# Two more operand sets, scans in place and a product tile of half the size in a chunked recurrence, with the inverse's contractions tied to steps

## The chip, the core and the metric

The kernel runs on one core of a Trainium2 chip. The metric is the device time of one execution in microseconds. The core's engines work side by side, each through its own instructions in order: TensorE (PE, with its weight loads shown as PEld), VectorE (DVE), ScalarE (ACT), GpSimd (POOL) and SyncE (SP), whose queue issues most of the DMAs. An instruction that waits holds up everything behind it on its engine or queue.

## The reference

A recurrence over 768 tokens for 4 batches of 8 heads with head dimension 40, and behind it a mixture of experts over all 3072 tokens.

```python
state = np.zeros((B, H, D, D), dtype=np.float32)
for t in range(S):
    y[:, :, t] = np.einsum('bhd,bhde->bhe', rt, state)
    Sa = np.einsum('bhde,bhe->bhd', state, at)
    state_decay = state * wt[:, :, None, :] - np.einsum('bhd,bhe->bhde', Sa, bt)
    state = state_decay + np.einsum('bhd,bhe->bhde', vt, kt)
...
x = np.ascontiguousarray(attn_out.transpose(0, 2, 1, 3)).reshape(B * S, H * D)
...
P = np.exp(logits)                      # logits = x @ w_gate, less the maximum
for _ in range(8):
    P /= P.sum(1, keepdims=True) + 1e-09
    P /= P.sum(0, keepdims=True) + 1e-09
    P *= N / E
for e in range(E):
    h = np.maximum(x @ w1[e], 0.0)
    ye = h @ w2[e]
    out += P[:, e:e + 1] * ye
```

## The kernel before

The recurrence is cut into 12 chunks of 64 tokens (c = 0 to 11). Within a chunk the dependence of one token on the next is solved by a triangular inverse, so that a chunk becomes a few small matrix products; only the state passes from chunk to chunk. Four pieces of work make up this stage.

**prep(c, b)** (L116 to L179) makes the operands of one chunk of one batch, 48 times in all; below, n = 4c + b is a prep's number. It loads the packed input into a tile inp (L119; from n = 8 on from a pool of two buffers), scans the running product of the decays forwards into q (L123, DVE), takes a reciprocal (L128) and scans backwards into gf (L133, DVE). gf goes out to memory as gd (L137, SP) and is read back later. POOL (for n of 8 and more) multiplies kb (L147) and the two halves of ab (L153, L154). TensorE forms the products ll (L159) and the transposes kt (L167), and ScalarE and VectorE copy the results into one of NSX = 20 operand sets: sx (L155, L156, L169, L174) and bb (L175, L176), with a small cc (L152). ScalarE also copies the strictly triangular part to lt (L173), which goes out to memory as ld (L178, on ScalarE's queue). Set n is used again by prep n + 20, so its tiles can be overwritten when step 3 of the recurrence of n has read bb.

**The inverse** of a pair of chunks (a segment s; eight preps belong to it) runs on VectorE. load_lu brings the eight ld back as lu, one small matrix in each partition (L367). inv_diag (L181) builds the inverses of the 8-wide diagonal blocks in seven short steps. inv_off (L198) joins two blocks of n with two products; contract (L189) makes each in two instructions, a multiply with the whole three-fold product into the tile pr (L193) and a sum over one index (L196). There are two joins of 8-blocks, of 512 products each, and one join of 16-blocks, done in four contractions of 2048, 1024, 1024 and 2048 products, so eight contractions in all. finish (L353) copies the inverse once transposed into pr (L356) and stores both as ud and nd (L358, L359).

**tload and tmat** read the pieces of the inverse for one chunk (L222 to L231, SP) and compute its remaining block with TensorE (gp L241, op L246) into tt.

**recur(c, b)** (L250) is the recurrence itself, a generator with five steps: loads of v, r, gr and vt (L253 to L259, SP), av and f (L269, DVE); xc (L276, PE) and its copies; pu (L287) and pm (L289, DVE), which need tt; c (L294, PE), ws (L296, DVE), y (L300, POOL) and z (L311, POOL until chunk 8, then DVE); and the transposed state vz (L316 to L319) for the next chunk. ScalarE also copies z into the next f (L264). Two buffers of y are stored as xd (L304).

**What sets the order.** Every piece gets an event time (L371 to L407), in which one step of the recurrence is one unit: step k of (c, b) stands at 5c + k + 1.1b. The instructions are traced in the order of these times, and a list scheduler with a timeline model then orders each engine: where an engine would be free it takes the ready instruction that was traced first, so that ready work with a late event time can be drawn forward into a gap. A segment that begins with chunk c0 has its preps from 5 c0 - 18 on, 0.75 apart, its load_lu right behind the last, and then the parts of the inverse 0.05 apart, so practically all at once. tload of a chunk stands at 5c - 0.5.

The recurrence ends at about 520 us; then the mixture of experts (from L476 on) fills TensorE. Its pools take over the memory of the recurrence's. pmat, ones and ident, which its normalization uses, have memory of their own throughout.

Of the kernel before, what the change touches and what calls it, by code (L numbers as in the profile page):

```python
# [11 lines left out]
F32 = mybir.dt.float32  # L12
# [17 lines left out]
def attention(ctx, tc, d, xd, ps, pq, pt, gs, lg):  # L30
    nc = tc.nc
    pin = ctx.enter_context(tc.tile_pool(name="a_in", bufs=1))
    inv = ctx.enter_context(tc.tile_pool(name="a_inv", bufs=1))
    sets = [ctx.enter_context(tc.tile_pool(name=f"a_set{i}", bufs=1)) for i in range(NSX)]
    const = ctx.enter_context(tc.tile_pool(name="a_const", bufs=1))
# [2 lines left out]
    dr = ctx.enter_context(tc.tile_pool(name="a_dr", bufs=2, space=bass.MemoryType.DRAM))  # L38
    dr1 = ctx.enter_context(tc.tile_pool(name="a_dr1", bufs=1, space=bass.MemoryType.DRAM))

    cst = const.tile([128, 64 + 64 + 104 + 128 + 40 + 260], F32, name="cst")
    nc.sync.dma_start(out=cst, in_=d["cst"])
    mask_u = cst[0:64, 0:64]
    mask_f = cst[0:R2, 64:128]
    mask_p = cst[:, 128:232]
    ident = cst[:, 232:360]
    one65 = cst[0:RP, 400:660]

    NTB = 2
    sx_b, bb_b, cc_b = ([None] * NSX for _ in range(3))  # L50
    raws = {}
    for n in range(NCH * NB - NSX, NCH * NB):
        i, pool = n % NSX, sets[n - NCH * NB + NSX]
# [20 lines left out]
    c1_b = [const.tile([R2, NP, 104], F32, name=f"c1{i}") for i in range(2)]  # L74
    unf = inv.tile([128, 1056], F32, name="un")
    luf = inv.tile([128, 1056], F32, name="lu")
    prf = inv.tile([128, 2048], F32, name="pr")
    gtf = inv.tile([128, 256], F32, name="gt")
    un, lu, tn = (t[:, 0:1024].rearrange("u (a b) -> u a b", b=32) for t in (unf, luf, prf))
    und, lud = (t.rearrange("u (b x) -> u b x", x=264)[:, :, 0:256].rearrange("u b (c j) -> u b c j", j=32)  # L80
# [19 lines left out]
    def first_use(i):  # L100
        if i in fresh:
            fresh.discard(i)
            nc.gpsimd.memset(bb_b[i], 0.0)
            nc.scalar.copy(out=sx_b[i][64:128].rearrange("r p h x -> r (p h) x")[:, :, 64:104],
                           in_=cst[64:128, 360:400].unsqueeze(1).broadcast_to([64, 8, 40]))

    state = {"sx": 0, "ab": 0, "g1": 0, "vz": 0, "c1": 0, "tt": 0, "f": 0, "rb": 0, "x1": 0}

# [7 lines left out]
    def prep(c, b, ld):  # L116
        cb = c * NB + b
        inp = raws[IN_MAP[cb]][0:RP, 0:1029] if IN_MAP.get(cb) else pin.tile([RP, 1029], F32, name="inp", bufs=2)
# [5 lines left out]
            out=qf.rearrange("r p t -> r (p t)"), data0=inp[:, 0:260], data1=one65,  # L124
# [4 lines left out]
        sx = rot("sx", sx_b)  # L129
        i = next(j for j in range(NSX) if sx_b[j] is sx)  # L130
        bb, cc = bb_b[i], cc_b[i]
        gf = pin.tile([RP, NP, 65], F32, name="gf", bufs=2)
        nc.vector.tensor_tensor_scan(  # L133
            out=gf.rearrange("r p t -> r (p t)")[:, 259::-1], data0=inp[:, 260:0:-1],
            data1=g1.rearrange("r p t -> r (p t)")[:, 259::-1], initial=0.0, op0=ALU.mult, op1=ALU.add)
        gd[c, b] = dr1.tile([RP, 260], F32, name=f"gd{cb}")
        nc.sync.dma_start(out=gd[c, b], in_=gf.rearrange("r p t -> r (p t)"))  # L137
        g = gf[0:R2, :, 64:0:-1]
        if cb < NKB:
            raw = raws[KB_SETS[cb % len(KB_SETS)]]  # L140
            kb = raw[0:R2, 0:512].rearrange("r (p k t) -> r p k t", p=NP, k=2)
            lt = raw[0:64, 512:1024].rearrange("r (p k t) -> r p k t", p=NP, k=2)
        else:
            kb = kb1
            lt = pin.tile([64, NP, 2, 64], F32, name="lt")
        eng = nc.vector if cb < NFAST else nc.gpsimd
        (nc.gpsimd if cb in KB_POOL else eng).tensor_tensor(  # L147
            out=kb[0:R2], in0=kb_in,
# [17 lines left out]
        for p in range(NP):  # L166
# [3 lines left out]
            out=sx[0:64, :, :, 0:64], in0=ll[0:64],  # L170
# [18 lines left out]
    def contract(us, dst, a, m):  # L189
        nu = us.stop - us.start  # L190
        n_c, n_r, n_k = a.shape[1], m.shape[2], a.shape[2]
        prv = prf[us, 0:n_c * n_r * n_k].rearrange("u (c k r) -> u c k r", r=n_r, k=n_k)
        nc.vector.tensor_tensor(  # L193
            out=prv, in0=a.unsqueeze(3).broadcast_to([nu, n_c, n_k, n_r]),
            in1=m.unsqueeze(1).broadcast_to([nu, n_c, n_k, n_r]), op=ALU.mult)
        nc.vector.tensor_reduce(out=dst, in_=prv.rearrange("u c k r -> u c r k"), op=ALU.add, axis=AX.X)  # L196

    def inv_off(us, o, n, h):  # L198
        gt = gtf[us, 0:n * n].rearrange("u (c r) -> u c r", r=n)
        un_, lu_ = un[us], lu[us]  # L200
        if h == n:
            contract(us, gt, un_[:, o:o + n, o:o + n], lu_[:, o:o + n, o + n:o + 2 * n])
            contract(us, un_[:, o:o + n, o + n:o + 2 * n], gt, un_[:, o + n:o + 2 * n, o + n:o + 2 * n])
            return
        contract(us, gt[:, 0:h], un_[:, o:o + h, o:o + n], lu_[:, o:o + n, o + n:o + 2 * n])
        contract(us, gt[:, h:n], un_[:, o + h:o + n, o + h:o + n], lu_[:, o + h:o + n, o + n:o + 2 * n])
        contract(us, un_[:, o:o + n, o + n:o + n + h], gt[:, :, 0:h], un_[:, o + n:o + n + h, o + n:o + n + h])
        contract(us, un_[:, o:o + n, o + n + h:o + 2 * n], gt, un_[:, o + n:o + 2 * n, o + n + h:o + 2 * n])

    INV = [(inv_diag, (i,)) for i in range(1, 8)] + [(inv_off, a) for a in ((0, 8, 8), (16, 8, 8), (0, 16, 8))]  # L210

    def tload(c):
        tt = rot("tt", tt_b)
# [36 lines left out]
    def recur(c, b):  # L250
# [9 lines left out]
                          in_=d["vt"][c, b].rearrange("s (g x) -> s g x", x=40))  # L260
# [6 lines left out]
        for p in range(NP):  # L267
            nc.tensor.matmul(av[:, p], lhsT=vz[:, p], rhs=rb[:, p], start=True, stop=True)
        nc.vector.tensor_tensor(  # L269
            out=f[0:R2, :, :, 0:64], in0=av,  # L270
# [28 lines left out]
        y = ys[c, b // 2]  # L299
        nc.gpsimd.tensor_tensor(out=y[:, :, b % 2], in0=ws[:, :, 0:64], in1=gr[0:R2, :, 64:0:-1], op=ALU.mult)  # L300
# [9 lines left out]
        z = wk.tile([R2, NP, 40], F32, name="z", bufs=4)  # L310
# [36 lines left out]

    def warm():
        fl = pt.tile([128, 512], F32, name="fl", tag="pt")
        for _ in range(4):  # L350
            nc.tensor.matmul(fl, lhsT=unf[:, 384:512], rhs=cst[:, 0:512], start=True, stop=True)

    def finish(s, us):  # L353
        if not s:
# [16 lines left out]
    ev = [(T_CLEAR, clear, ())]  # L371
# [11 lines left out]
    for c in range(NCH):  # L383
# [3 lines left out]
        t = 5 * c + 2 - T_LEAD  # L387
# [3 lines left out]
    for s, cs in enumerate(GROUPS):  # L391
        us = slice(0, 64 * len(cs))
        t0 = 5 * cs[0] - 10
        n = len(cs) * NB
        for i in range(n):
            cb = (cs[0] + i // NB, i % NB)
            j = cb[0] * NB + cb[1] - NSX
            t = 5 * (j // 4) + 3 + SKEW * (j % 4) + 0.01
            t = max(t, t0 + P0 + PD * i) if s else -20 + 0.01 * i
            ev.append((t, do_prep, (s,) + cb + (i == 0,)))  # L400
        t += 0.02
        ev.append((t, load_lu, (s, len(cs))))
        for i, (fn, a) in enumerate(INV):
            ev.append((t + INV_DT * i, fn, (us,) + a))
        ev.append((t + INV_DT * 10 + 0.01, finish, (s, us)))
    for _, fn, args in sorted(ev, key=lambda x: x[0]):
        fn(*args)  # L407
    while gq:
# [5 lines left out]
GRP = {c: (i, j) for i, g in enumerate(GROUPS) for j, c in enumerate(g)}  # L414
P0 = -8
PD = 0.75
INV_DT = 0.05
SKEW = 1.1
NSX = 20
GL = 1  # L420
NY = 2
NGR = 2
NFB = 3
NRB = 2
KB_POOL = (1,2,3,4,5,6,7)
IN_SETS = (19, 18, 17, 16)
KB_SETS = (15, 14, 13, 12)
IN_SEQ = (19,18,17,16,0,0,19,18)
IN_MAP = dict(enumerate(IN_SEQ))
N_SP = 8  # L430
NKB = 8
# [23 lines left out]
def body(ctx, tc, d, out):  # L455
    nc = tc.nc
# [2 lines left out]
    xv = xd.rearrange("(k r) (s u c) -> s u r k c", k=2, u=3, c=256)  # L459

    one = ctx.enter_context(tc.tile_pool(name="one", bufs=1))
    pmat = one.tile([128, 24, E], F32, name="pmat")
    lg = one.tile([128, 24, E], F32, name="lg")
    ones = one.tile([128, 128], F32, name="ones")
    ident = one.tile([128, 128], F32, name="ident")
    gs = one.tile([R2, NP, E], F32, name="gs")

    with ExitStack() as actx:
        ps, pq, pt = (actx.enter_context(tc.tile_pool(name=f"a_ps{i}", bufs=n, space=bass.MemoryType.PSUM))
                      for i, n in enumerate((PC, PQ, PT)))  # L470
        nc.sync.dma_start(out=gs, in_=d["gate"])
        attention(actx, tc, d, xd, ps, pq, pt, gs, lg)
        nc.gpsimd.memset(ones, 1.0)
        nc.sync.dma_start(out=ident, in_=d["cst"][:, 232:360])

    stg = ctx.enter_context(tc.tile_pool(name="stg", bufs=2))  # L476
    x0 = ctx.enter_context(tc.tile_pool(name="x0", bufs=1))
    hp = ctx.enter_context(tc.tile_pool(name="hp", bufs=2))
# [279 lines left out]
def _layout(inputs):  # L758
# [18 lines left out]
    x = split(g["r"])  # L777
# [14 lines left out]
    wg = g["moe_w_gate"].reshape(NP, 2, D, E).transpose(1, 2, 0, 3)  # L792
    gate = np.zeros((R2, NP, E), np.float32)
    gate[0:40], gate[64:104] = wg[0], wg[1]
    cst = np.zeros((128, 660), np.float32)
    i = np.arange(64)
    up = (i[:, None] < i[None, :]).astype(np.float32)
    cst[0:64, 0:64] = up
    cst[0:64, 64:128] = up
    cst[64:128, 64:128] = 1.0  # L800
    cst[0:64, 128:192] = up
    cst[64:128, 128:192] = up
    cst[:, 192:232] = 1.0
    cst[:, 232:360] = np.eye(128)
    cst[64:104, 360:400] = np.eye(40)
    cst[:, 400::65] = 1.0
# [20 lines left out]
```

## Time and profile before

| | us |
|---|---|
| median of 3 runs | 1840.97 |
| lowest and highest | 1838.9 and 1845.11 |
| the profiled execution's own time | 1844.61 |
| its span in the profile | 1842.7 |
| VectorE idle, 193 to 238 us | 0.15 |
| VectorE idle, 238 to 268 us | 14.47 |

A line of a group reads: source line, engine, operation, tile written and tiles read, shapes, count, then busy time and mean ns, then the idle time before it and what ended that. A line of a timeline begins with start and duration in us. A line of the waits gives who waited for whom, the total in us, how often, and the longest. A row of a stretch gives from and to, the length, and per engine the busy time and in brackets the count of instructions, then the granted TensorE clock, the share of DMA and GB/s. A line of the chain gives start, length and what it was.

### The profile page before, as it was taken

To read this page: it belongs to the slowest core of one execution; us is meant where nothing else is said; L and a number is where in the kernel's file an instruction comes from. 1 tells how busy PE (TensorE), PEld (TensorE's weight loads), DVE (VectorE), ACT (ScalarE), POOL (GpSimd) and SP (SyncE) were. 2 spreads that over 40 slices of the span, in tenths; PEclk is the share of its full clock that TensorE was granted. 3 is DMA by queue.
4 is the path that set the end of the run, shared out by engine and by line. 5 is a ranking of instruction groups with operands and counts; after the bars stand their busy time and mean duration, and the time that the engine had idled before them with its cause. 6 is when DMAs were issued, how large, how long until landed. Compare 5 with 4: busy or idle time off the path is not lost.

```text
span 1842.7 us, 31504 instructions
## 1 busy us (share of the span) xinstructions
PE 1732.1 (94%) x11851; PEld 1697.6 (92%) x11851; DVE 1387.3 (75%) x2319; ACT 856.0 (46%) x1848; POOL 857.4 (47%) x844
## 2 busy tenths in 40 slices
PE   5488888899989999999999999999999999999999
PEld 4378888888889999999999999999999999999999
DVE  8876968877688768677776868977686877777676
ACT  6346667665643534344343433445343443425342
POOL 6545545532662617355371826007191744628170
PEclk8579899999899999999999999999999999999999
DMA  8467887875820102011110202201020111102001
GB/s 215 128 151 165 188 182 184 183 175 130 207 74 31 57 4 71 22 53 39 37 58 17 76 19 69 65 12 57 19 75 20 56 38 38 57 19 75 6 33 43
DMA packets 194957, 145.10 MB, mean 79 GB/s; under 512 B 143861, under 2 KB 171637, under 8 KB 194805
## 3 DMA queue, kind: packets, MB, share of 16 engines
q1 hardware_dynamic: 189013, 137.09, 28.7%
q10 hardware_dynamic: 5792, 6.00, 1.2%
q8 instruction: 94, 1.54, 0.3%
q14 instruction: 58, 0.48, 0.1%
HBM read 117.00 MB, written 26.04 MB: 78 GB/s over the span
## 4 chain that ended last, share of the span: by engine, by line
PE 73%; DVE 13%; DMA 7%; issue 3%; ACT 2%; POOL 1%; SPq 1%; ACTq 0%; DVEq 0%; POOLq 0%
PE op L636 36%; PE p L571 33%; DVE pr L193 2%; DVE un L196 2%; DMA inp<-in_inp_dram 2%; DVE gt L196 1%; DVE q L123 1%; DMA ld<-lt 1%; DMA lu<-ld 1%; DVE gf L133 1%; DMA td<-nd 1%; PE pu L287 1%; PE ll L159 1%; DMA rb<-in_r_dram 1%; DVE pm L289 1%
## 5 line engine op out<-in xcount | busy, mean ns | idle before, releaser
L571 PE MATMUL p<-xch,wh 128*128 128x384 f32 (+1 forms) x1792 | 604.8, 339 | 8.9 <-DVE sm L589 5.2
L592 ACT ACTIVATE hh<-sm 128x384 fp32r<-128x384 f32 x512 | 269.5, 527 | 725.3 <-DVE sm L589 725.3
L636 PE MATMUL op<-wh,hh 128*128 128x320 f32 x1536 | 476.8, 311 | 1.0 <-ACT hh L592 0.9
L636 PE MATMUL op<-wl,hh 128*128 128x320 f32 x1536 | 474.7, 310 | 0.0
L636 PE MATMUL op<-wh,hl 128*128 128x320 f32 x1536 | 467.3, 310 | 0.8 <-DVE hl L595 0.8
L517 POOL TENSOR_TENSOR wl<-ws,wh 128x640 fp32r<-128x640 f32 x60 | 103.0, 1716 | 608.3 <-ACT wh L515 608.2
L595 DVE SCALAR_TENSOR_TENSOR hl<-sm,hh 128x384 fp32r<-128x384 f32 x512 | 371.1, 758 | 2.4 <-ACT hh L592 2.0
L571 PEld LDWEIGHTS p<-xch,wh 128*128 128x128 f32 (+1 forms) x1792 | 337.2, 188 | 12.6 <-DVE sm L589 6.3
L571 PE MATMUL p<-xcl,wh 128*128 128x384 f32 x896 | 302.5, 338 | 0.0
L571 PE MATMUL p<-xch,wl 128*128 128x384 f32 x896 | 301.7, 337 | 0.0
L636 PEld LDWEIGHTS op<-wh,hh 128*128 128x128 f32 x1536 | 290.2, 189 | 1.6 <-ACT hh L592 1.5
L636 PEld LDWEIGHTS op<-wl,hh 128*128 128x128 f32 x1536 | 291.0, 189 | 0.0
L636 PEld LDWEIGHTS op<-wh,hl 128*128 128x128 f32 x1536 | 287.2, 188 | 1.1 <-DVE hl L595 1.0
L589 DVE TENSOR_TENSOR sm<-p,u 128x384 f32<-128x384 f32 x384 | 233.1, 617 | 8.8
L589 DVE TENSOR_TENSOR sm<-p,p 128x384 f32<-128x384 f32 x128 | 71.3, 557 | 129.8 <-PE p L571 76.3
L571 PEld LDWEIGHTS p<-xcl,wh 128*128 128x128 f32 x896 | 168.7, 188 | 0.0
L571 PEld LDWEIGHTS p<-xch,wl 128*128 128x128 f32 x896 | 168.6, 188 | 0.0
L589 DVE TENSOR_TENSOR p<-p,p 128x384 f32<-128x384 f32 x128 | 71.2, 556 | 102.6 <-PE p L571 102.2
L589 DVE TENSOR_TENSOR u<-p,p 128x384 f32<-128x384 f32 x128 | 70.9, 554 | 59.4 <-PE p L571 58.2
L525 POOL TENSOR_TENSOR wl<-ss,wh 128x512 fp32r<-128x512 f32 x60 | 89.7, 1496 | 28.3 <-ACT wh L522 24.2
L300 POOL TENSOR_TENSOR y<-ws,gr 104x256 f32<-104x256 f32 x48 | 47.1, 980 | 113.1 <-DVE ws L296 99.9
L700 DVE SCALAR_TENSOR_TENSOR acc<-op,pmat,acc 128x320 f32<-128x320 f32 x168 | 91.3, 544 | 4.5 <-PE op L636 4.4
(160 smaller groups left out, 2717.4 us busy)
## 6 DMA issues: line engine op xcount, KB each, us to landing
ws<-in_wts_dram SPq DMA_DIRECT2D x60, 832.0 KB
inp<-in_inp_dram SPq DMA_DIRECT2D x42, 450.2 KB
rb<-in_r_dram SPq DMA_DIRECT2D x48, 224.0 KB
gd<-gf SPq DMA_DIRECT2D x48, 113.8 KB
gr<-gd SPq DMA_DIRECT2D x48, 113.8 KB
vz<-in_v_dram SPq DMA_DIRECT2D x48, 112.0 KB
ld<-lt ACTq DMA_DIRECT2D x40, 128.0 KB
f<-in_vt_dram SPq DMA_DIRECT2D x48, 80.0 KB
```

What stands on the lines that cost most here:

```text
L123: nc.vector.tensor_tensor_scan(out=qf.rearrange("r p t -> r (p t)"), data0=inp[:, 0:260], data1=one65, initial=0.0, op0=ALU.mult, op1=ALU.add)
L193: nc.vector.tensor_tensor(out=prv, in0=a.unsqueeze(3).broadcast_to([nu, n_c, n_k, n_r]), in1=m.unsqueeze(1).broadcast_to([nu, n_c, n_k, n_ ...
L196: nc.vector.tensor_reduce(out=dst, in_=prv.rearrange("u c k r -> u c r k"), op=ALU.add, axis=AX.X)
L300: nc.gpsimd.tensor_tensor(out=y[:, :, b % 2], in0=ws[:, :, 0:64], in1=gr[0:R2, :, 64:0:-1], op=ALU.mult)
L517: g.tensor_tensor(out=wl[:, 0:640], in0=raw[:, 256:896], in1=wh[:, 0:640], op=ALU.subtract)
L525: g.tensor_tensor(out=lv[:, 3:7], in0=so[:, :, 0], in1=hv[:, 3:7, 0], op=ALU.subtract)
L571: nc.tensor.matmul(o, lhsT=w_, rhs=x_, start=(j == 0), stop=(j == 3))
L589: eng.tensor_tensor(out=out, in0=x, in1=y, op=ALU.add)
L592: nc.scalar.activation(out=hh[:, f, h], in_=sm[f][:, h], func=AF.Relu)
L595: v.scalar_tensor_tensor(out=hl[:, f, h], in0=sm[f][:, h], scalar=0.0, in1=hh[:, f, h], op0=ALU.max, op1=ALU.subtract)
L636: nc.tensor.matmul(ops[i], lhsT=a[:, h, cs], rhs=w_[:, cw], start=(f == 0 and h == 0 and j == 0), stop=(last and h == 1 and j == 2))
L700: nc.vector.scalar_tensor_tensor(out=acc[:, m], in0=ops[i], scalar=pmat[:, n, e:e + 1], in1=acc[:, m], op0=ALU.mult, op1=ALU.add)
```

## The change

- NSX goes from 20 to 22. The sets that lend their memory to the first preps (IN_SETS, KB_SETS, IN_SEQ) move along.
- Room for them: the backward scan writes in place into inp, so gf is a part of inp, and gd is stored from there. From n = 8 on lt lies in inp too, over the k and b that kb has been made of. The product tile pr goes from 2048 to 1024 columns. Two masks become one, and the identity of the first use of a set is cut from the large one. pmat, ones and ident get memory only after the recurrence; the load of ident and the fill of ones move behind it.
- The joins of the inverse are ten contractions, each with at most 1024 products: four for the joins of 8, and six for the join of 16 (1024, 768, 1024, 1024, 768, 1024).
- Their event times are spread. From the second segment on they lie 0.44 units apart for the first four and 0.94 for the last six; the last stands 7.2 units behind load_lu and finish 7.9 behind it.
- From the second segment on, ahead of each contraction, `after` copies one element of a z into a corner of pr. It is the z of the latest step that stands at least one unit earlier in the event list, if there is one. Since the contraction writes pr, it can't be put ahead of that copy, nor the copy ahead of that z.

```diff
-    prf = inv.tile([128, 2048], F32, name="pr")
+    prf = inv.tile([128, 1024], F32, name="pr")
...
-        gf = pin.tile([RP, NP, 65], F32, name="gf", bufs=2)
+        gf = inp[:, 1:261].rearrange("r (p t) -> r p t", p=NP)
         nc.vector.tensor_tensor_scan(
-            out=gf.rearrange("r p t -> r (p t)")[:, 259::-1], data0=inp[:, 260:0:-1],
+            out=inp[:, 260:0:-1], data0=inp[:, 260:0:-1],
...
-        nc.sync.dma_start(out=gd[c, b], in_=gf.rearrange("r p t -> r (p t)"))
+        nc.sync.dma_start(out=gd[c, b], in_=inp[:, 1:261])
...
-            lt = pin.tile([64, NP, 2, 64], F32, name="lt")
+            lt = inp[0:64, 261:773].rearrange("r (p k t) -> r p k t", p=NP, k=2)
...
+        m, e = o + n, o + 2 * n
+        if part:
+            contract(us, un_[:, o:m, m + x:m + y], gt[:, :, 0:y], un_[:, m:m + y, m + x:m + y])
+        else:
+            contract(us, gt[:, x:y], un_[:, o + x:o + y, o + x:m], lu_[:, o + x:m, m:e])
+
+    INV = [(0.06 * i, inv_diag, (i,)) for i in range(1, 8)]
+    INV += [(0.5 + 0.35 * i, inv_off, (o, 8, 0, 8, i % 2)) for i, o in enumerate((0, 0, 16, 16))]
+    INV += [(2.0 + 0.75 * i, inv_off, (0, 16, x, y, i // 3))
+            for i, (x, y) in enumerate(((0, 4), (4, 8), (8, 16), (0, 8), (8, 12), (12, 16)))]
...
+        zs[c, b] = z
...
+    def after(t):
+        at = {5 * c + 3 + SKEW * b: z for (c, b), z in zs.items() if 5 * c + 3 + SKEW * b <= t - GATE}
+        if at:
+            nc.vector.tensor_copy(out=prf[0:1, 0:1], in_=at[max(at)][0:1, 0, 0:1])
...
-            nc.tensor.matmul(fl, lhsT=unf[:, 384:512], rhs=cst[:, 0:512], start=True, stop=True)
+            nc.tensor.matmul(fl[:, 0:296], lhsT=unf[:, 384:512], rhs=cst[:, 0:296], start=True, stop=True)
...
-        for i, (fn, a) in enumerate(INV):
-            ev.append((t + INV_DT * i, fn, (us,) + a))
-        ev.append((t + INV_DT * 10 + 0.01, finish, (s, us)))
+        for dt, fn, a in INV:
+            ti = t + dt * (INV_DT if s else 0.1)
+            if s and fn is inv_off:
+                ev.append((ti - 0.001, after, (ti,)))
+            ev.append((ti, fn, (us,) + a))
+        ev.append((t + 6.3 * (INV_DT if s else 0.1), finish, (s, us)))
...
-INV_DT = 0.05
+INV_DT = 1.25
+GATE = 1.0
 SKEW = 1.1
-NSX = 20
+NSX = 22
...
+    mid = ctx.enter_context(tc.tile_pool(name="mid", bufs=1))
+    pmat = mid.tile([128, 24, E], F32, name="pmat")
+    ones = mid.tile([128, 128], F32, name="ones")
+    ident = mid.tile([128, 128], F32, name="ident")
+    nc.gpsimd.memset(ones, 1.0)
+    nc.sync.dma_start(out=ident, in_=d["cst"][:, 168:296])
```

More of the change, by code (lines that the diff above doesn't have):

```diff
@@ L39, in attention @@
     dr1 = ctx.enter_context(tc.tile_pool(name="a_dr1", bufs=1, space=bass.MemoryType.DRAM))
-    cst = const.tile([128, 64 + 64 + 104 + 128 + 40 + 260], F32, name="cst")
+    cst = const.tile([128, 64 + 104 + 128 + 260], F32, name="cst")
     nc.sync.dma_start(out=cst, in_=d["cst"])
     mask_u = cst[0:64, 0:64]
[L44 to L47, printed above, removed]
+    mask_f = cst[0:R2, 0:64]
+    mask_p = cst[:, 64:168]
+    ident = cst[:, 168:296]
+    one65 = cst[0:RP, 296:556]
     NTB = 2
@@ L104, in first_use @@
             nc.scalar.copy(out=sx_b[i][64:128].rearrange("r p h x -> r (p h) x")[:, :, 64:104],
-                           in_=cst[64:128, 360:400].unsqueeze(1).broadcast_to([64, 8, 40]))
+                           in_=ident[64:128, 64:104].unsqueeze(1).broadcast_to([64, 8, 40]))
     state = {"sx": 0, "ab": 0, "g1": 0, "vz": 0, "c1": 0, "tt": 0, "f": 0, "rb": 0, "x1": 0}
@@ L196, in contract, with inv_off @@
         nc.vector.tensor_reduce(out=dst, in_=prv.rearrange("u c k r -> u c r k"), op=ALU.add, axis=AX.X)
-    def inv_off(us, o, n, h):
+    def inv_off(us, o, n, x, y, part):
         gt = gtf[us, 0:n * n].rearrange("u (c r) -> u c r", r=n)
         un_, lu_ = un[us], lu[us]
[L201 to L210, printed above, removed]
+        m, e = o + n, o + 2 * n
[7 more added lines that the diff above has]
+            for i, (x, y) in enumerate(((0, 4), (4, 8), (8, 16), (0, 8), (8, 12), (12, 16)))]
     def tload(c):
@@ L338, in gate_step @@
                 gq.popleft()
+    zs = {}
+    def after(t):
+        at = {5 * c + 3 + SKEW * b: z for (c, b), z in zs.items() if 5 * c + 3 + SKEW * b <= t - GATE}
+        if at:
+            nc.vector.tensor_copy(out=prf[0:1, 0:1], in_=at[max(at)][0:1, 0, 0:1])
     gq, gcount = deque(), [0]
@@ L349, in warm @@
         fl = pt.tile([128, 512], F32, name="fl", tag="pt")
-        for _ in range(4):
-            nc.tensor.matmul(fl, lhsT=unf[:, 384:512], rhs=cst[:, 0:512], start=True, stop=True)
+        for _ in range(7):
+            nc.tensor.matmul(fl[:, 0:296], lhsT=unf[:, 384:512], rhs=cst[:, 0:296], start=True, stop=True)
     def finish(s, us):
@@ L425 @@
 KB_POOL = (1,2,3,4,5,6,7)
-IN_SETS = (19, 18, 17, 16)
-KB_SETS = (15, 14, 13, 12)
-IN_SEQ = (19,18,17,16,0,0,19,18)
+IN_SETS = (21, 20, 19, 18)
+KB_SETS = (17, 16, 15, 14)
+IN_SEQ = (21, 20, 19, 18, 0, 0, 21, 20)
 IN_MAP = dict(enumerate(IN_SEQ))
@@ L461, in body @@
     one = ctx.enter_context(tc.tile_pool(name="one", bufs=1))
-    pmat = one.tile([128, 24, E], F32, name="pmat")
     lg = one.tile([128, 24, E], F32, name="lg")
-    ones = one.tile([128, 128], F32, name="ones")
-    ident = one.tile([128, 128], F32, name="ident")
     gs = one.tile([R2, NP, E], F32, name="gs")
@@ L472, in body @@
         attention(actx, tc, d, xd, ps, pq, pt, gs, lg)
-        nc.gpsimd.memset(ones, 1.0)
-        nc.sync.dma_start(out=ident, in_=d["cst"][:, 232:360])
+    mid = ctx.enter_context(tc.tile_pool(name="mid", bufs=1))
[4 more added lines that the diff above has]
+    nc.sync.dma_start(out=ident, in_=d["cst"][:, 168:296])
     stg = ctx.enter_context(tc.tile_pool(name="stg", bufs=2))
@@ L794, in _layout @@
     gate[0:40], gate[64:104] = wg[0], wg[1]
-    cst = np.zeros((128, 660), np.float32)
+    cst = np.zeros((128, 556), np.float32)
     i = np.arange(64)
@@ L798, in _layout @@
     cst[0:64, 0:64] = up
+    cst[64:128, 0:64] = 1.0
     cst[0:64, 64:128] = up
[L800 to L806, printed above, removed]
+    cst[64:128, 64:128] = up
+    cst[:, 128:168] = 1.0
+    cst[:, 168:296] = np.eye(128)
+    cst[:, 296::65] = 1.0
     arrays = dict(inp=inp, r=rb.reshape(NCH, NB, RP, NP, 128), v=packed(g["v"]),
```

## Prediction

> **What bounds the kernel now.** I read the page's head first, then the table by stretch, then the groups of VectorE by shape, then the timelines of single engines around one prep.
>
> ```profile
> span 1842.7 us, 31504 instructions
> ```
>
> The execution took 1844.61 us, so 1.9 us lie around this span; the median of the three runs, 1840.97, is 3.6 us below it. The mixture of experts behind about 520 us is full of TensorE work and the change does not touch its code. So the question is the recurrence, from about 110 to 500 us. Its rows give per stretch: length, then busy time and count of PE, PEld, DVE, ACT and POOL, then granted clock, DMA share and GB/s.
>
> ```profile
> 110.00:157.00 47.00, 43.10 (x380) 40.55 (x381) 41.73 (x53) 29.38 (x74) 27.23 (x26) 0.85 0.70 159
> 193.00:238.00 45.00, 41.27 (x382) 39.16 (x383) 44.85 (x60) 31.76 (x81) 24.21 (x29) 0.93 0.81 185
> 238.00:268.00 30.00, 24.60 (x236) 22.87 (x235) 15.53 (x34) 20.19 (x51) 12.75 (x20) 0.93 0.83 176
> 268.00:313.00 45.00, 40.94 (x380) 38.67 (x380) 44.97 (x60) 30.96 (x79) 23.85 (x30) 0.93 0.80 189
> 313.00:343.00 30.00, 24.65 (x236) 23.12 (x236) 15.92 (x35) 20.56 (x52) 12.57 (x20) 0.93 0.86 183
> 343.00:387.00 44.00, 38.87 (x374) 36.62 (x373) 43.97 (x58) 30.04 (x76) 23.41 (x29) 0.97 0.79 185
> 387.00:412.00 25.00, 23.71 (x237) 22.05 (x237) 11.96 (x30) 18.10 (x47) 6.80 (x11) 1.00 0.74 159
> 410.00:443.00 33.00, 32.16 (x310) 29.86 (x309) 32.83 (x35) 18.63 (x48) 7.78 (x9) 0.95 0.50 113
> ```
>
> The pattern repeats every 75 us, once for each pair of chunks: 45 us in which VectorE has no idle time at all (44.85 of 45), because the whole inverse lies there, and 30 us in which it is half idle (15.53 of 30). The stretch 387 to 412 shows what TensorE does with less in its way: 237 matmul records in 25 us, 9.48 a us. The bursts reach 382 / 45 = 8.49, the quiet stretches 236 / 30 = 7.87. So neither half runs at TensorE's pace; the burst is bound by VectorE. In the quiet half the wait that stands out is VectorE's for the prep's input, between 120 and 500 us (total, times, longest):
>
> ```profile
> DVE q L123 <- DMA inp<-in_inp_dram: 20.7, 6, 5.2
> ```
>
> **Part 1, the smaller product tile.** These are the eight instructions of the block of 16 (mean ns stands behind the bar and the busy time), and the small copy that is nearest to the tie:
>
> ```profile
> L196 DVE TENSOR_REDUCE un<-pr 128x128 f32<-128x2048 f32 x5 | 19.2, 3846 | 0.0
> L196 DVE TENSOR_REDUCE gt<-pr 128x128 f32<-128x2048 f32 x5 | 18.2, 3631 | 0.0
> L193 DVE TENSOR_TENSOR pr<-un,lu 128x2048 f32<-128x2048 f32 x5 | 12.2, 2450 | 0.0
> L193 DVE TENSOR_TENSOR pr<-gt,un 128x2048 f32<-128x2048 f32 x5 | 11.4, 2277 | 0.0
> L196 DVE TENSOR_REDUCE un<-pr 128x128 f32<-128x1024 f32 x5 | 9.9, 1985 | 0.0
> L196 DVE TENSOR_REDUCE gt<-pr 128x128 f32<-128x1024 f32 x5 | 9.5, 1893 | 0.0
> L193 DVE TENSOR_TENSOR pr<-un,lu 128x1024 f32<-128x1024 f32 x5 | 6.5, 1302 | 0.0
> L193 DVE TENSOR_TENSOR pr<-gt,un 128x1024 f32<-128x1024 f32 x5 | 6.0, 1209 | 0.0
> L330 DVE COPY lg<-lp 128x8 f32<-128x8 f32 x21 | 3.2, 151 | 0.5 <-PE lp L326 0.5
> ```
>
> The eight sum to 18.59 us. The new code has six contractions, four of 1024 products and two of 768. A pair of 1024 is 1.30 + 1.89 = 3.19 us. From 2048 to 1024 a multiply falls by 1.12 ns an element and a reduce by 1.70, so a pair of 768 is 3.19 - 256 x 2.82 ns = 2.47. Together 4 x 3.19 + 2 x 2.47 = 17.7 us, 0.9 less per inverse: 4.5 us over the five inverses after the first, and 0.9 in the prologue, where the first inverse stands on the chain. The ties cost 0.15 us each; by the event times there are ten for each of the last four inverses and one for the second, 41 in all, 6.2 us. VectorE gets 6.2 - 4.5 = 2 us more, which I put on the path because it is full there.
>
> **Part 2, the burst.** At 9.48 records a us the five bursts would be shorter by 6.9, 4.7, 4.9, 4.5 and 0.3 us, 21 us in all: the most that spreading can give in them. The quiet stretches would add 5.1 each, but they are not made of VectorE work. What do the ties hold back? A step of the recurrence is one unit of the event list. The four contractions of 8 stand within 1.3 units of each other and stay a burst; the six of the 16-block are 0.94 units apart and tied to a z at least one unit older. They are 17.7 us of about 25, so I take 0.7 of 21: 15 us gained. The other end is nothing, by these rows of the inverse for chunks 4 and 5:
>
> ```profile
> 173.40 1.91 SPq L367 DMA_DIRECT2D lu<-ld  x4
> 169.90 0.69 DVE L269 TENSOR_TENSOR f<-av,cst 104x512 f32<-104x512 f32 x1 [2.60 <-PE av L268]
> 198.42 0.45 POOL L311 TENSOR_TENSOR z<-ws,st 104x160 f32<-104x160 f32 x1
> 225.20 2.27 DVE L193 TENSOR_TENSOR pr<-gt,un 128x2048 f32<-128x2048 f32 x1
> ```
>
> Its operands are loaded at 173.4, when chunk 2 has just begun (f at 169.9, unit 10), while its event stands at unit 20 - 18 + 7 x 0.75 = 7.3. The last of its new ties, at 7.3 + 1.25 x 5.75 = 14.5, waits for the z of chunk 2, batch 0, which is there at 198.9; the last product starts at 225.2. At this lag every tie is open long before it is reached, and only the order of priority changes.
>
> The lag would shrink if preps came earlier, for which the two more sets are there. Set reuse as it stands, for the prep of chunk 7, batch 0 and the step that frees its set:
>
> ```profile
> 192.78 1.72 PE L294 MATMUL c<-pm,bb 128*104 128x104 f32 x8 [1.88 <-ACT c L283]
> 221.51 0.30 ACT L175 ACTIVATE bb<-kt 64x160 f32<-64x160 f32 x1
> ```
>
> The set is free at 194.5 and rewritten at 221.5: 27 us of slack on the chip. What more sets can give comes through the scheduler's order alone. I count nothing for it by itself.
>
> **Part 3, scans and lt in place.** The input tile has two buffers. Today it is free after the last POOL product; afterwards gd and lt lie in it and it is held until both stores have landed. Rows for the prep with its input issued at 202.52 and for its forerunner in the same buffer (first the release, then the issue, the forerunner's lt store, and this prep's first scan); then two later preps:
>
> ```profile
> 201.82 0.67 POOL L154 TENSOR_TENSOR ab<-inp,gf 40x256 f32<-40x256 f32 x1
> 202.52 0.33 SPq L119 DMA_DIRECT2D inp<-in_inp_dram  x1
> 207.21 0.45 ACTq L178 DMA_DIRECT2D ld<-lt  x1
> 209.17 1.16 DVE L123 TENSOR_TENSOR_SCAN q<-inp,cst 112x260 f32<-112x260 f32 x1
> 219.00 0.43 SPq L119 DMA_DIRECT2D inp<-in_inp_dram  x1
> 228.40 0.68 DVE L123 TENSOR_TENSOR_SCAN q<-inp,cst 112x260 f32<-112x260 f32 x1
> 242.38 0.45 ACTq L178 DMA_DIRECT2D ld<-lt  x1
> 253.29 0.70 DVE L123 TENSOR_TENSOR_SCAN q<-inp,cst 112x260 f32<-112x260 f32 x1 [2.79 <-DMA inp<-in_inp_dram]
> ```
>
> and two pieces of the chain (start, length):
>
> ```profile
> 256.59 5.25 DMA inp<-in_inp_dram
> 289.83 2.21 DMA ld<-lt
> ```
>
> The issue at 202.52 follows the release at 202.49: this buffer already paces the loads. With the change it would wait for 207.2 + 2.2 = 209.4 and be usable 5.3 us later, at 214.7 instead of 209.2: 5.5 us late. On SP's queue stand behind it the loads of r, v and gr for the next steps. Eight preps are two chains of four; three links of each lie in the burst, 3 x 5.5 = 16.5 us, and the fourth has slack, 253.3 - (242.4 + 2.2 + 5.3) = 3.4. So 13 us a pair of chunks and 52 over the four pairs is the upper end. The lower end is nothing, since in the burst the landed input waits for VectorE anyway: 228.4 - 219.0 - 5.3 = 4.1 us at the later prep, 1.4 at the earlier. With 4.1 absorbed, 3 x 1.4 - 3.4 = 0.8 is left per pair, 3 us in all; with 1.4, 36. Where the ties bind VectorE is freer and the prep itself shorter, so I stay near the small end: 6 us lost.
>
> **Part 4, the rest.** The merged masks and seven matmuls of 296 columns for four of 512 are the same work. ident, ones and pmat now lie where attention's tiles were; ident's first use is late,
>
> ```profile
> L656 PE MATMUL mp<-ident,mxs x1: 271/271/271, 523.7 to 523.7; 128*1 128x128 f32 x1
> ```
>
> so the recurrence's tail covers its load; uncovered it would cost less than the 5.25 us of the larger inp load.
>
> **A rule against the rows.** VectorE's products and POOL's steps disturb each other:
>
> ```profile
> 280.63 2.70 DVE L193 TENSOR_TENSOR pr<-un,lu 128x2048 f32<-128x2048 f32 x1
> 281.14 2.73 POOL L300 TENSOR_TENSOR y<-ws,gr 104x256 f32<-104x256 f32 x1
> 218.95 0.68 POOL L300 TENSOR_TENSOR y<-ws,gr 104x256 f32<-104x256 f32 x1
> ```
>
> A y beside a 2048-product took 2.73 us, one without it 0.68. The total time of the products hardly changes, so I count nothing. The Trainium skill, "SBUF — State Buffer", section "SBUF: two separate sides", has these two engines share one port pair as an exclusive lock, and the loser blocks for the whole instruction; the 2.73 agrees. By that rule halving a product halves the longest block, an estimated 1 us for each of five inverses, and the time would be 1828.
>
> **The sum.** Prologue -1, VectorE +2, burst -15, input buffers +6: -8 us, 1836.6 against this execution, 1833 against the median. A measurement here can tell about 0.3%, 5.5 us, from no change.
>
> **Rivals.** First, slower: the input buffer paces the preps. Two buffers carry eight preps in 75 us if each is held for 18.75 us. The input issued at 219.0 has its lt landed at 242.4 + 2.2 = 244.6, 25.6 us. If the new schedule doesn't bring this under 18.75, the preps come late, the inverse with them, and every pair of chunks waits. At half the upper end: +26, no burst gain, +2, -1: 1868. For it: the issue on the very heels of the release. Against: fewer preps in flight wait less for each other.
>
> Second, also slower: the ties hold VectorE. It is in order, so behind a copy that waits for z stand the f, pm and ws of the other batches. Today ScalarE pays such a wait:
>
> ```profile
> ACT f L264 <- POOL z L311: 26.9, 14, 4.3
> ```
>
> Over 44 z that is 0.61 us each; 41 ties make 25 us, so -8 + 25 = +17: 1858. It needs ties that bind, as the forecast does; against it stands the lag of Part 2.
>
> Third, the change doesn't do what it says: the ties are open, the sets had slack, the burst stays, the buffers are absorbed: 1841, within 5.
>
> **Chances.** Forecast, 1833 with 1809 to 1835: 0.43, its lower end with the full 21 and both quiet stretches' 10. Nothing: 0.17. Input buffer: 0.28, from 1847 to 1893. Ties that hold: 0.12. So faster 0.43, same 0.17, slower 0.40. The range reaches from 1808 to 1868, the middle of the first rival.
>
> **What would show it.** Right: VectorE's full stretches gone or under 40 us, with 9 records a us in them; q starting within 2 us of its input's landing; the ties with under 0.2 us of idle before them. The first rival: SP's waits for ld<-lt ahead of the input loads far above today's, and preps over 10 us apart. The second: VectorE idle before the tie's copy, released by POOL's z. I am wrong in the main step if the bursts stay 45 us long.

## The result and the profile after

The changed kernel takes 1888.26 us (median; 1884.28 to 1889.39), 1.0252 times the kernel before, with a 95% interval of 1.0234 to 1.027. The forecast of 1833 was wrong, also in its sign, and the time lies above the range. The first rival came true, the input buffer that paces the preps, near the upper end of its range (1847 to 1893).

The span grew from 1842.7 to 1885.4 us, by 42.7. A row of one source line gives how often it ran, the shortest, median and longest duration in ns, and the first and the last start in us. Before, for the loads of the inputs (L119) and the first vector product of each step of the recurrence (L269):

```profile
L119 SPq DMA_DIRECT2D inp<-in_inp_dram x42: 312/416/637, 3.5 to 373.9; - x42
L269 DVE TENSOR_TENSOR f<-av,cst x48: 649/680/704, 20.2 to 507.6; 104x512 f32<-104x512 f32 x48
```

After, the same two lines:

```profile
L119 SPq DMA_DIRECT2D inp<-in_inp_dram x42: 312/333/572, 3.5 to 427.5; - x42
L269 DVE TENSOR_TENSOR f<-av,cst x48: 654/678/712, 22.2 to 550.6; 104x512 f32<-104x512 f32 x48
```

The last input is asked for 53.6 us later and the last f comes 43.0 us later; behind that f lie 1842.7 - 507.6 = 1335.1 us before and 1885.4 - 550.6 = 1334.8 us after, so the mixture of experts took no part. All of the loss lies in the recurrence, and the inputs are late ahead of it. From the input of n = 8 to that of n = 47 there are 39 intervals: 8.83 us each before, 10.15 after.

The table by stretch of the kernel after, over its inverses and the stretches between them, in the columns of the prediction:

```profile
121.00:172.00 51.00, 44.06 (x372) 41.88 (x373) 46.62 (x70) 32.03 (x81) 25.25 (x32) 0.87 0.68 151
211.00:253.00 42.00, 34.25 (x287) 32.12 (x286) 40.46 (x62) 24.83 (x65) 20.79 (x26) 0.82 0.60 139
253.00:293.00 40.00, 32.87 (x270) 30.76 (x270) 21.57 (x44) 23.70 (x59) 16.98 (x23) 0.85 0.88 181
293.00:341.00 48.00, 44.19 (x383) 42.26 (x383) 43.23 (x67) 30.35 (x78) 24.51 (x31) 0.84 0.69 146
341.00:376.00 35.00, 27.30 (x249) 25.80 (x248) 18.38 (x39) 19.71 (x50) 13.47 (x18) 0.91 0.82 185
376.00:421.00 45.00, 39.32 (x352) 37.17 (x352) 40.20 (x65) 28.95 (x75) 22.26 (x26) 0.88 0.71 149
```

The inverses are still bursts of 42 to 51 us, with VectorE 89 to 96% busy, but TensorE gets less done in them: 7.3, 6.8, 8.0 and 7.8 records a us, where it had 8.49. The stretches between them, 30 us long before, are now 35 to 40, with 5 to 14% more work in them (270 and 249 matmul records against 236).

SyncE's waits, from 0 to 560 us (total, times, longest), the costliest three:

```profile
SPq L137 <- DVE inp L133: 56.4, 27, 5.5
SPq L119 <- DMA ld<-inp: 48.4, 21, 7.2
SPq L257 <- POOL y L300: 34.2, 17, 8.1
```

The second row is new: the load of an input waits for the store of an earlier prep's lt. In the waits of all engines from 100 to 560 us, what hangs on the input has grown (q's wait for it was 20.7 us in six times before):

```profile
POOL kb L147 <- DVE q L123: 70.2, 14, 10.3
DVE q L123 <- DMA inp<-in_inp_dram: 42.6, 19, 6.4
```

One round of one buffer shows the loop: the timelines of SP, VectorE and ScalarE, each line a start and a duration, for the preps 36 and 38.

```profile
310.60 0.32 SPq L119 DMA_DIRECT2D inp<-in_inp_dram  x1
314.82 0.92 DVE L123 TENSOR_TENSOR_SCAN q<-inp,cst 112x260 f32<-112x260 f32 x1 [0.82 <-POOL y L300]
327.92 0.47 ACTq L178 DMA_DIRECT2D ld<-inp  x1
331.30 0.33 SPq L119 DMA_DIRECT2D inp<-in_inp_dram  x1
335.13 0.70 DVE L123 TENSOR_TENSOR_SCAN q<-inp,cst 112x260 f32<-112x260 f32 x1
```

The scan starts 4.2 us behind the issue of its input, with VectorE idle for the last 0.8 of them, lt goes out 13.1 us behind the scan, and the buffer's next input is issued 3.4 us behind that, as soon as SyncE's wait for the store has ended (at 331.23): 20.7 us. With two buffers that is a prep every 10.35 us. The means over n = 8 to 45, from the same three lines of each trace:

| us | issue to scan | scan to lt's store | store to the buffer's next input | round |
|---|---|---|---|---|
| before | 7.8 | 14.6 | -4.5 | 17.9 |
| after | 4.9 | 11.4 | +4.2 | 20.4 |

Before, the next input was issued 4.5 us ahead of the store, and its scan came 7.8 us behind the issue, some us after the landing. After, the issue comes behind the store, and the scan 4.9 us behind the issue, about as long as a landing takes (5.25 us for the load in the prediction's chain).

In 21 of these 38 rounds, the count in the row of the waits, SyncE stood waiting for the store: it landed 2.2 to 5.1 us behind its issue, 2.8 on the mean, and the input was issued 0.1 us later. In the other 17 the input was issued 5.7 us behind the store on the mean, without a wait for it: SyncE came to this load late, straight from other entries of its queue.

### The profile page after: what moved, and what is told of

The parts are those of the page before. It is cut to its first block, busy times and chain, and to the rows that moved or that the text cites. A ratio compares the mean times of both kernels' runs of the same rounds, so it can differ in the third digit from the quotient of the medians.

```text
span 1885.4 us, 31593 instructions
## 1 busy us (share of the span) xinstructions
PE 1751.8 (93%) x11857; PEld 1718.1 (91%) x11857; DVE 1400.4 (74%) x2384; ACT 856.3 (45%) x1850; POOL 856.8 (45%) x846
## 4 chain that ended last, share of the span: by engine, by line
PE 70%; DVE 4%; issue 1%; DMA 1%; SPq 1%; ACT 1%; POOL 0%; ACTq 0%; DVEq 0%; POOLq 0%
PE op L649 35%; PE p L584 33%; DVE hl L608 0%; DVE sm L602 0%; PE c L294 0%; PE pu L287 0%; PE av L268 0%; DVE u L602 0%; SPq L253 0%; DMA rb<-in_r_dram 0%; PE xc L276 0%; DVE xcl L570 0%; DVE xch L567 0%; DVE un L196 0%; DVE pr L193 0%
## 5 line engine op out<-in xcount | busy, mean ns | idle before, releaser
L584 PEld LDWEIGHTS p<-xch,wh 128*128 128x128 f32 (+1 forms) x1792 | 337.1, 188 | 13.1 <-DVE sm L602 6.3
L147 POOL TENSOR_TENSOR kb<-inp,q 104x512 f32<-104x512 f32 x40 | 50.5, 1263 | 124.7 <-DVE q L123 82.4
L159 PE MATMUL ll<-ab,kb 128*128 128x128 f32 x320 | 59.5, 344 | 44.5 <-POOL ab L154 43.0
```

Source lines behind the costliest of these rows:

```text
L147: (nc.gpsimd if cb in KB_POOL else eng).tensor_tensor(out=kb[0:R2], in0=kb_in, in1=q[:, :, 63::-1].unsqueeze(2).broadcast_to([R2, NP, 2, 6 ...
L159: nc.tensor.matmul(ll[:, p], lhsT=kb[:, p], rhs=ab[0:kb.shape[0], p], start=True, stop=True)
L584: nc.tensor.matmul(o, lhsT=w_, rhs=x_, start=(j == 0), stop=(j == 3))
```

## The experiments

Theory A is the first rival: lt in the input tile lengthens the hold of a buffer, and the pace of the preps sets the time. It has two forms, the pace itself, or SyncE's queue standing still with the loads of the recurrence behind it. Theory B was formed on the trace of after: a tie is a reader of a z, z rotates through four buffers, and a later z can't be written until the tie has read the older one in its buffer. From the timelines of VectorE and POOL:

```profile
174.44 1.28 POOL L311 TENSOR_TENSOR z<-ws,cc 104x160 f32<-104x160 f32 x1
217.06 0.14 DVE L346 COPY pr<-z 1x1 f32<-1x1 f32 x1
218.99 0.45 POOL L311 TENSOR_TENSOR z<-ws,cc 104x160 f32<-104x160 f32 x1
```

and from the answer on the tie's line, first who it is, then who waited for it most (us, times):

```profile
L346 DVE COPY pr<-z x41: 116/131/143, 164.1 to 483.5; 1x1 f32<-1x1 f32 x41
...
  POOL z L311: 14.3, 3
```

The z at 218.99 comes 44.6 us behind the one ahead of it and 1.8 us behind the third tie of that inverse; the z at 301.1, 382.2 and 459.0 us come 0.1 to 0.4 us behind the end of a tie. By B the recurrence waits for these ties.

The runs with lt in a tile of its own or with more buffers have 21 sets or 20 to make room (NSX, with the lists of lending sets moved along), and one run is the changed kernel with 21 sets. Times are medians, ratios are to the kernel before on the same chip.

**Only the place of lt, on the kernel before** (before_lt_in):

```diff
-            lt = pin.tile([64, NP, 2, 64], F32, name="lt")
+            lt = inp[0:64, 261:773].rearrange("r (p k t) -> r p k t", p=NP, k=2)
```

> The kernel before with one line of the change alone: lt of preps 8 and later lies in the input tile. Theory A (the input buffer that is held to the landing of the lt store paces the preps) expects it to be slower by 35 us or more, 1876 to 1900 us, with preps about 10 us apart in place of 8.8 and SP's input loads waiting for the ld store as in the changed kernel (48.4 us in 21 waits). The rival, that the loss of the changed kernel needs several of its parts together (in-place scans, ten contractions, spread times), expects less than 20 us.

Measured 1909.82 us, 1.0373 [1.0356, 1.0391]. This one line alone costs 70 us, more than the whole change and more than theory A had expected. The rows of its loads and its last f:

```profile
L119 SPq DMA_DIRECT2D inp<-in_inp_dram x42: 312/334/601, 3.5 to 446.4; - x42
L269 DVE TENSOR_TENSOR f<-av,cst x48: 652/678/695, 20.6 to 568.5; 104x512 f32<-104x512 f32 x48
```

and SyncE's wait for lt's store, of which the kernel before has none:

```profile
SPq L119 <- DMA ld<-inp: 56.4, 24, 5.8
```

The last input is 72.5 us late, the last f 60.9; a prep starts every 10.67 us, and a round of a buffer takes 21.5 (4.9, 12.8 and +3.7). There is no tie in it and no set more.

**The change without lt's place, and the same with it** (lt_own_21, sets21):

```diff
 # lt_own_21
-            lt = inp[0:64, 261:773].rearrange("r (p k t) -> r p k t", p=NP, k=2)
+            lt = pin.tile([64, NP, 2, 64], F32, name="lt")
 # both
-NSX = 22
+NSX = 21
```

> The changed kernel with lt in a tile of its own again, so that the input buffer is free when the last product and the gd store are done, and 21 sets to make room; the ties stay. Theory A expects SP's waits of the input load for the ld store (48.4 us in 21 waits) to vanish, preps about 9 us apart and 1840 to 1855 us. Theory B expects z of chunk 1, batch 3 still right behind the third tie of its inverse; since the inverse comes a little earlier with faster preps, 1860 to 1880 us.

> The changed kernel with 21 sets in place of 22 and nothing else: the control for the two runs that had to give up a set. Both theories expect no more than 6 us of difference from 1888, since a set stood free for 27 us before it was written again in the kernel before. If sets do pace the preps, it is slower by 8 us or more.

lt_own_21 takes 1827.17 us, 0.9921 [0.9904, 0.9939], and sets21 1889.14, 1.0263 [1.0245, 1.0281]. So the set makes no difference to the loss, and lt's place costs 62 us. Of the two forecasts for lt_own_21, A's has the direction, but the time lies below both. The loads of lt_own_21, SyncE's longest wait ahead of them, and two inverses in the table by stretch:

```profile
L119 SPq DMA_DIRECT2D inp<-in_inp_dram x42: 317/328/1056, 3.5 to 360.5; - x42
```

```profile
SPq L119 <- DMA gd<-inp: 33.9, 24, 3.6
```

```profile
179.00:230.00 51.00, 44.52 (x412) 40.77 (x410) 47.87 (x78) 35.53 (x90) 35.35 (x40) 0.97 0.83 189
247.00:290.00 43.00, 39.22 (x371) 36.96 (x369) 42.73 (x67) 30.38 (x78) 25.70 (x29) 0.96 0.89 191
```

Inputs are 8.46 us apart. The backward scan in place does lie in the input tile here, and SyncE waits 33.9 us for its store, but the round is 17.0 us (6.5, 14.1 and -3.6): gd goes out early in a prep, lt at its end. These two bursts are about as full of VectorE's work as before the change (47.87 of 51 us and 42.73 of 43).

**A third input buffer** (inp3_21), lt still in it:

```diff
-        inp = raws[IN_MAP[cb]][0:RP, 0:1029] if IN_MAP.get(cb) else pin.tile([RP, 1029], F32, name="inp", bufs=2)
+        inp = raws[IN_MAP[cb]][0:RP, 0:1029] if IN_MAP.get(cb) else pin.tile([RP, 1029], F32, name="inp", bufs=3)
-NSX = 22
+NSX = 21
```

> The changed kernel with a third input buffer and 21 sets; lt and the scans stay in place and the ties stay. If the pace of the buffers is the cause, three buffers of about 19 us carry a prep every 6.3 us, less than is needed, so the time falls to that of the run with lt in its own tile (1827) or below, 1815 to 1835 us. If instead the store of lt out of the input tile is slow by itself, or the order of the queues is at fault, it stays above 1860.

Measured 1839.64 us, 0.9994 [0.9982, 1.0006], 49.5 less than sets21. It misses its own range by 4.6 us and stays 12.5 above lt_own_21; what these are isn't shown. SyncE's wait and the loads:

```profile
SPq L119 <- DMA ld<-inp: 41.9, 19, 4.7
```

```profile
L119 SPq DMA_DIRECT2D inp<-in_inp_dram x42: 312/333/1125, 3.5 to 371.4; - x42
```

The round is longer than ever, 27.0 us, but three buffers share it: 8.94 us a prep. SyncE still waits 41.9 us for lt's stores, against 49.6 in sets21. So the queue's wait isn't what costs; the pace is. Of A's two forms this leaves the first, in which the order of the queue still has a share of the round (the 17 late issues above).

**Without the ties, and with eight z buffers** (no_ties with 22 sets, z8_21 with 21):

```diff
 # no_ties
-            if s and fn is inv_off:
-                ev.append((ti - 0.001, after, (ti,)))
 # z8_21
-        z = wk.tile([R2, NP, 40], F32, name="z", bufs=4)
+        z = wk.tile([R2, NP, 40], F32, name="z", bufs=8)
```

> The changed kernel without the 41 copies that tie a contraction to a z; 22 sets, scans and lt in place, ten contractions and their event times stay. Theory A, the input buffer: two buffers that are held until the lt store has landed pace the preps at 10 us apart, so without ties the preps stay about 10 us apart (31.5 to 427.5 us over 39 issues in the changed kernel) and the time stays at 1875 to 1888 us. Theory B, the ties hold z: a tie of the inverse reads a z that is two or more steps old, and the next z in the same one of four buffers waits for it; chunk 2 took 67 us from f to f against 44.6 before because z of chunk 1, batch 3 came at 219.0, right behind the tie at 217.1. Without ties that wait goes, chunk 2 falls to about 45 us and the time to 1840 to 1855 us.

> The changed kernel with eight buffers of z in place of four, and 21 sets in place of 22 to make room; the ties stay. Theory B (a tie holds a z buffer that the next chunk needs) expects what it expects without ties, 1840 to 1855 us, since with eight buffers the z that a tie reads isn't needed again for ten units; z of chunk 1, batch 3 would come within 12 us of its neighbour. Theory A (input buffer) expects 1875 to 1888. A third theory, that a tie stops VectorE until z is there, expects idle time of VectorE before the ties; in the changed kernel it is 0.04 us at most, so it expects little to move here.

no_ties takes 1886.96 us, 1.0249 [1.0234, 1.0265], no different from the change; z8_21 1900.92, 1.032 [1.0297, 1.0342], 11.8 more than sets21 and above what either theory expected. B falls as the cause of the time. Its wait is there all the same: with it gone, the chunk in which it lay is shorter, and others are longer. Length of a chunk, from its first f to that of the next, and the last f:

| us | chunk 2 | chunk 4 | chunk 10 | last f |
|---|---|---|---|---|
| sets21 | 67.0 | 44.9 | 32.8 | 547.0 |
| z8_21 | 47.2 | 54.9 | 53.7 | 558.6 |
| no_ties | 41.4 | 58.7 | 35.7 | 549.2 |

The recurrence runs ahead and then waits for the next inverse, which comes no sooner than its preps (the last input of no_ties is issued at 435.9 us, of the change at 427.5). z8_21 loses its 11.6 us at the last one: VectorE's and TensorE's timelines there,

```profile
495.37 1.03 DVE L364 COPY pr<-un 128x1024 f32<-128x1024 f32 x1
503.02 1.94 PE L241 MATMUL gp<-td,lg 64*64 64x64 f32 x16 [11.79 <-DMA td<-nd]
509.60 0.17 DVE L331 COPY lg<-lp 128x8 f32<-128x8 f32 x1 [13.20 <-PE lp L327]
```

where finish copies the inverse out at 495.4 (485.7 in sets21) and both engines stand for 12 to 13 us until it has been out to memory and back. Its inputs are only 4.0 us later (the last at 429.7 against 425.7); why that inverse is 9.7 later stays open.

**The ties with the pace restored** (lt_own_21_no_ties): lt_own_21 less the two lines of no_ties.

> The run with lt in its own tile and 21 sets, without the 41 ties. That run took 1827.2 us, 13 below the kernel before. If the ties make that gain by keeping contractions back, this one comes out at 1836 to 1845 us with VectorE full for 40 us and more per pair of chunks; if the ties do nothing, as the lag of 3 to 4 units suggests, it stays within 6 us of 1827.

Measured 1833.55 us, 0.9956 [0.9942, 0.997]. This lies between its two forecasts. Against lt_own_21 the ties bring 6.4 us here (the two intervals don't meet), where under the slow pace they brought nothing.

**What the scan in place and the sets bring.** ties_20_own keeps only the inverse's part of the change (ten contractions, their spread, the ties, the product tile) with 20 sets and gf and lt in tiles of their own; lt_own_20 has 20 sets and the scan in place; ties_21_own has 21 sets and both in tiles of their own.

```diff
 # ties_20_own, ties_21_own
-        gf = inp[:, 1:261].rearrange("r (p t) -> r p t", p=NP)
+        gf = pin.tile([RP, NP, 65], F32, name="gf", bufs=2)
```

> Ten contractions of at most 1024 products with spread times and ties on 20 sets, with gf and lt in tiles of their own as in the kernel before: what the inverse's part of the change does without its memory part. If the gain of the run with lt in its own tile comes from the inverse's part, this is 1820 to 1832 us; if it came from the 21st set, 1836 to 1845 us.

> The best run so far (lt in its own tile, scans in place, ties, 21 sets, 1827.2 us) with 20 sets. With 20 sets and gf in its own tile the same inverse took 1837.6, so the 10 us between the two come from the 21st set or from the scan in place. If from the set, this is 1834 to 1842; if from the scan in place, within 4 us of 1827.

> The same with 21 sets and both gf and lt in tiles of their own: the other corner of the square of set count and place of gf. If the set gives the 10 us, 1824 to 1831; if the scan in place does, 1834 to 1842. The scan in place holds the input until the gd store has landed (33.9 us of SP's waits in the best run so far), so by theory A gf in its own tile can't be slower.

| median us, ratio [95%] | gf in the input tile | gf in its own |
|---|---|---|
| 20 sets | 1831.91, 0.9953 [0.9938, 0.9967] | 1837.64, 0.9983 [0.9973, 0.9992] |
| 21 sets | 1827.17, 0.9921 [0.9904, 0.9939] | 1827.93, 0.9939 [0.9925, 0.9953] |

One set more brings about 5 us with the scan in place (the intervals just touch) and 10 without. So ties_20_own and ties_21_own came out as the set would have it, and lt_own_20 between its two forecasts. The inverse's part alone, on 20 sets, is worth 2.5 us. With 21 sets the scan's place does nothing; with 20 it is 6 us better in place, though a tile of its own frees the input sooner. Why that is stays open.

**A third buffer where lt is out of it** (lt_own_20_inp3, own_20_inp3): lt_own_20 and ties_20_own with bufs=3 for inp.

> lt in its own tile, scans in place, ties, 20 sets and a third input buffer. If input buffers still pace the preps there (33.9 us of SP's waits for the gd store), the third buffer takes that away and it beats its twin with two buffers by 5 us or more; if not, within 4 us of it.

> The inverse's part of the change on 20 sets with gf and lt in their own tiles (1837.6 us) and a third input buffer. In the kernel before, 9 input loads between 120 and 500 us waited 13.7 us in all for the last POOL product; a third buffer takes those waits. Theory A expects 2 to 10 us less than 1837.6; if the pace of preps is set by VectorE and POOL there, no change.

1833.64 us, 0.9968 [0.9953, 0.9984], against 1831.91 without the third buffer: nothing. And 1830.29, 0.9942 [0.9927, 0.9956], against 1837.64: 7 us better. With lt elsewhere a third buffer is worth 7 us at most, where with lt in it it is worth 50.

The best of these kernels is lt_own_21, 13.4 us (0.8%) below the kernel before and 61 below the change.

## Why the prediction was wrong

**What bounds the kernel.** Half right. VectorE does fill the inverses, and still does in the fastest kernel. But I took the wait of q for its input in the quiet half, 20.7 us, as what stands out there, and didn't ask what it says of the next change: the inputs had little to spare, a buffer went round in 17.9 us on the mean, 18.75 was the need, and there was next to nothing to give.

**Part 1** held. These groups of VectorE, from 120 to 560 us, are the multiplies of 1024 products, two of their four reduces, the four instructions of 768, and the ties:

```profile
L193 DVE TENSOR_TENSOR pr<-un,lu 128x1024 f32<-128x1024 f32 x10 | 12.8, 1276 | 0.1
L193 DVE TENSOR_TENSOR pr<-gt,un 128x1024 f32<-128x1024 f32 x10 | 12.7, 1274 | 0.1
L196 DVE TENSOR_REDUCE un<-pr 128x128 f32<-128x1024 f32 x5 | 10.0, 1996 | 0.0
L196 DVE TENSOR_REDUCE gt<-pr 128x64 f32<-128x1024 f32 x5 | 9.5, 1895 | 0.0
L193 DVE TENSOR_TENSOR pr<-un,lu 128x768 f32<-128x768 f32 x5 | 6.0, 1206 | 0.0
L193 DVE TENSOR_TENSOR pr<-gt,un 128x768 f32<-128x768 f32 x5 | 4.8, 954 | 0.0
L196 DVE TENSOR_REDUCE un<-pr 128x64 f32<-128x768 f32 x5 | 7.7, 1546 | 0.0
L196 DVE TENSOR_REDUCE gt<-pr 128x64 f32<-128x768 f32 x5 | 7.3, 1457 | 0.0
L346 DVE COPY pr<-z 1x1 f32<-1x1 f32 x41 | 5.5, 134 | 0.5
```

A pair of 1024 is 1.28 + 1.95 = 3.22 us (forecast 3.19), a pair of 768 is 1.08 + 1.50 = 2.58 (2.47); six contractions 18.0 (17.7). There are 41 ties of 134 ns, 5.5 us (6.2). VectorE gets 5.5 - 5 x 0.55 = 2.7 us more; I had 2.

**Part 2** failed too, by the sign that I had set for it: the bursts stayed. In lt_own_21, the fastest, the three in the middle last 43 to 51 us, VectorE is busy for 42.73 of 43 in the fullest, and they reach 7.8 to 8.6 records a us, not 9. Where the inverse's part stands alone, in ties_20_own, it gains 2.5 us, where -1 + 2 - 15 makes -14. That lt_own_21 gains 13.4 is close to this sum by luck: as single steps from that run 6.4 us come from the ties and 4.7 from the 21st set, for which I counted nothing; the remaining 2 are not taken apart. "Every tie is open long before it is reached" held, with 0.5 us of idle ahead of 41 ties, so the second rival fell. What I didn't see is the tie's other end: being a reader, it keeps a buffer of z from being written, 20 us in chunk 2. It cost nothing in the end only because the inverse was later still.

**Part 3 is the step that failed**: "so I stay near the small end: 6 us lost". The runs put 62 us (lt_own_21 to sets21) and 70 us (on the kernel before) in its place; even the upper end of 52 was short of these. Three things were mis-sized. A link: by the row that I used the next input is issued 6.9 us later (209.4 in place of 202.5), and the means say 8.7, from 4.5 ahead of lt's store to 4.2 behind it. What absorbs it: the 5.5 us of a link had the 1.4 us for which the landed input waited for VectorE taken off already, and I took 1.4 or 4.1 off again; taken off once, the 4.1 leave 3 x (6.9 - 4.1) - 3.4 = 5.0 us a pair of chunks, 20 in all where I had 3. In the mean issue to scan went from 7.8 to 4.9, so 2.9 were absorbed at each link; with the prep's own 3.2 (14.6 to 11.4) that leaves 8.7 - 6.1 = 2.6 us a round, 1.3 a prep, and 39 preps make 51 (53.6 at the last input). And the fourth link's slack, which I took off once in each pair of chunks, was no gift: a wait that exists because the buffer is ahead is gone as soon as the buffer is behind, everywhere at once. The loss against lt_own_21 is larger since that kernel's preps come every 8.46 us: (10.14 - 8.46) x 39 = 65.5 us, and the last input of sets21 is 65.2 later (425.7 against 360.5).

**The first rival** named the right row and the right sign ("preps over 10 us apart": 10.15). Its condition was drawn too narrowly: it compared the hold alone with 18.75 us. Counted as there, with 2.2 us for the store to land, the mean hold did fall under it, to 18.4. But the next issue comes 4.2 us behind the store, not 2.2: where SyncE waited for the store, 2.9 (2.8 for the landing and 0.1), and in the other 17 rounds 5.7. 18.4 + 2.0 = 20.4 is the round, and it is over 18.75. The late issues are an estimated (5.7 - 2.9) x 17 / 38 = 1.3 us of it; what SyncE's order is worth in the time was not measured apart. Taking half the upper end for its time had no reason in the rows. Nor does the forecast's lower end, 1809, come out of its terms: with the full 21, both quiet stretches' 10 and no loss at the buffers the sum is 1841 - 1 + 2 - 21 - 10 = 1811.

**Part 4** held, as the unchanged 1335 us behind the last f show. On the rule set against the rows: the longest and the median y (L300) before,

```profile
L300 POOL TENSOR_TENSOR y<-ws,gr x48: 673/686/2731, 122.7 to 517.0; 104x256 f32<-104x256 f32 x48
```

and after:

```profile
L300 POOL TENSOR_TENSOR y<-ws,gr x48: 675/682/1772, 124.0 to 560.6; 104x256 f32<-104x256 f32 x48
```

The longest fell by 0.96 us with a product tile of half the size; it ran beside a product of 1024 that took 1.2 us, and ended 0.5 us behind it, as a y of 2.73 us did behind its product of 2048 before. The Trainium skill, "SBUF — State Buffer", section "SBUF: two separate sides", lets the loser of the port lock wait for the whole instruction, and the rows agree. Whether it is worth the 1 us per inverse estimated from it is not shown, since no run changes the tile's size alone.

## What to carry to other kernels

When a result is put into an input's tile to save memory, the buffer is held to the landing of the last store from it. Add up one whole round (issue, landing, work, store, landing, next issue), divide by the number of buffers, and compare it with the pace that the kernel needs; don't set today's waits against it, since they end as soon as the buffer is late. A dependence added for its order also has a second end: it is one more reader, and keeps what it reads from being overwritten.

## What was not expected of the hardware

TensorE's granted clock was lower with the late preps: in the inverses from the second on 0.82 to 0.88 after, 0.93 to 0.97 before, and 0.89 to 1.00 in lt_own_21. In the 20 us around the tie that held the z of 218.99, TensorE was busy for 10.23 us and had half its clock:

```profile
200.00:220.00 20.00, 10.23 (x61) 9.31 (x62) 15.08 (x34) 6.80 (x18) 8.39 (x9) 0.50 0.64 116
```

The Trainium skill, "TensorE: Matmul & The Clock Gate", section "Part 1: The HAM clock gate", has the clock set by how busy TensorE was lately, with half speed as the default. The 0.50 agrees. So late preps go with a slower clock behind them; how much of the 62 us that is was not measured apart.
